# Mamba2 + SwiGLU on one core: four of the eight whole gate/value tiles of block 0 go to three parts, weight passes spread over three engines, a new step order

## The chip, the cores and the metric

One core of one Trainium2 chip runs the whole program as a single launch. The metric is the device time of that launch in microseconds (us); the time before is 364.84 us, the median of three runs (364.48 to 365.87). The engines are named as in the profile: PE (TensorE matmul), PEld (its weight loads), DVE (VectorE), ACT (ScalarE), POOL (GpSimd), SP (SyncE, which issues nearly all loads and stores).

## The reference

Two stages, fp32 in and out. The first is a Mamba2 state-space scan over 4 batches, 8 heads, 768 steps; the second is a SwiGLU feed-forward over the 3072 resulting rows.

```python
# scan, per batch and head; D = 32, N = 16, chunks of 32
log_a = np.log(np.clip(a, 1e-6, 1.0)); cum = np.cumsum(la)           # within a chunk
L = np.exp(cum[i] - cum[j]) * causal
y = ((C @ B.T) * L) @ x  +  (C @ state) * np.exp(cum)
state = np.exp(sum(la)) * state + sum_j(B_j x_j * exp(cum[-1] - cum[j]))
# feed-forward, x = y as (3072, 256); w_gate, w_val: 256 x 1536; w_out: 1536 x 256
xn  = x / sqrt(mean(x*x) + 1e-6) * rms_g
out = (silu(xn @ w_gate) * (xn @ w_val)) @ w_out
```

## The kernel before

**Tiling.** The 3072 rows are 6 blocks of 512 columns (`blk` 0 to 5), each made of two pairs (`p`) of two 128-step chunks. For each block the scan comes first (`gb` products of C and B, `L` decays times products, `A` and `S` the states, `yi` and `ya` the outputs), then the norm (`sq`, `ms`, `rs`, `xn`), then the feed-forward: for each of 12 slices `f` of 128 hidden rows a gate tile (`m` = 0) and a value tile (`m` = 1), each 128x512 in one PSUM bank, `silu` on ACT and `hid` on DVE, and the output products `O`.

**Whole and split tiles.** A tile can be made in two ways. `F` (`gv_whole`, line 1149) multiplies the fp32 weight by the fp32 activation: two matmuls in the program, which the profile records as four. `X` (`gv_split`, line 1159) multiplies three reduced-precision (fp32r) parts: `xh` with `wh`, `xl` with the low half of `wp`, `xk` with the mixed half of `wp`, two matmuls each, six in all. `X` needs six tiles made beforehand: three parts of the activation (`xH`, `xL`, `xK`) and three of the weight (`wH`, `wL`, `wM`). The set `GV4` lists the tiles of block 0 that are whole; besides them slices 0 and 1 of block 0 are made early from the un-normed activation (`early`, line 1112). Block 0's output products (`OF`, line 1234) are all whole, those of other blocks (`OX`, line 1228; `OY`, line 1206) are split.

**Weights.** A piece `k` of the weights (0 to 11 gate and value, 12 to 17 output) is loaded as 16-bit words (`fetch`, on SP) and rebuilt in fp32: `pow` makes a power of two on ACT (two instructions, line 272), `man` makes the mantissa on DVE (line 300), `wt` puts them together on DVE (line 306). Then the parts: `wH` on ACT (line 328) or `wHv` on DVE (line 331), `wL` and `wM` on DVE (line 322).

**The order of the work.** There is no scheduler. One string, `order`, of 1200 steps is written out by hand or by a program outside; each step calls the function of its name and so appends its instructions to the queues of its engines. Each engine takes its queue strictly in that order and waits on semaphores. Steps read `group:name.numbers`: `b:X.0.7.0` is the split gate tile of block 0, slice 7. A step names its engine by its ending: `xL` DVE, `subp` and `hLp` POOL, `hH` ACT, `hHv` DVE.

**Buffers.** `Ring` hands out places of one pool in the order in which they were freed (`free.pop(0)`), at build time. The PSUM banks are the ring `one`, eight of them. So which earlier step a tile must wait for, to get its bank, also follows from the order string.

**The place around the change.** After the common first 150 steps PE makes whole tiles of block 0, the products `gb.1` of pairs 2 and 3, the state products `A.2` and `A.3` (line 830, which read the loaded `x` of pairs 2 and 3 and the scaled `Bd`, and write two PSUM banks each), and the outputs `yi`, `ya` of these pairs (line 916). `Td.3` (`turned_decayed`, line 734, DVE) multiplies a transposed tile by the decays `dT` that SP loads (line 722); it is also the last reader of the bank of `turn.3`.

Of the kernel before, what the change touches and what calls it, by code (L numbers as in the profile page):

```python
# [50 lines left out]
def kernel(  # L51
# [12 lines left out]
    nc = tc.nc  # L64
# [237 lines left out]

    def weight(k):
# [13 lines left out]
    def weight_part(k, i):  # L317

        shape = fetched[k][2]
        if k not in low_parts:  # L320
            split_parts(k)
        nc.vector.scalar_tensor_tensor(  # L322
            out=(low_parts, mixed_parts)[i][k], in0=high_parts[k], scalar=(-UP, GAIN)[i],
            in1=view(ws[k], shape), op0=ALU.mult, op1=(ALU.add, ALU.subtract)[i])
        ws[k].used()
# [40 lines left out]
    kinks = const.tile([P, 2], FP32, name="kinks")  # L366
# [60 lines left out]
    def kinks_of_powers():  # L427
        for k, v in enumerate((-896.0, -1792.0 * 128.0)):
            nc.vector.memset(kinks[:, k:k + 1], v)
# [237 lines left out]
    def scale(p):  # L667
# [3 lines left out]
        for name, src, d in (("Cd", "C", to_i), ("Bd", "B", from_j))[0 if p < 2 else 1:]:  # L671
            s[name + "b"] = k1.take(1, name)
            s[name] = view(s[name + "b"], [P, 2, NH, N])
            nc.vector.tensor_tensor(
# [52 lines left out]
    def turned_decayed(p):  # L727
        if p in SQUARES:
            T = transposed(p)[:, :, 3]
            nc.vector.tensor_tensor(out=T, in0=T, in1=st[p]["dT"], op=ALU.mult)  # L730
# [340 lines left out]
    def x_part(blk, t, i):  # L1071

        xparts[blk, t, i] = b = h.take(modes(blk).count(3), "x" + "hlk"[i])
        part_of(view(b, [P, TB], F32R), xns[blk][1][:, t], view(xparts[blk, t, 0], [P, TB]), i)
# [12 lines left out]
    GV4 = {(0, 2, 0), (0, 3, 0), (0, 4, 0), (0, 4, 1), (0, 5, 0), (0, 5, 1), (0, 6, 0), (0, 7, 0)}  # L1087
# [228 lines left out]
    def token_out():  # L1316
# [23 lines left out]
        "pow": power, "man": mantissa, "wt": weight,  # L1340
        "wH": lambda k: weight_high(k, by_scalar),
        "wHv": lambda k: weight_high(k, by_vector),
        "wL": lambda k: weight_part(k, 0), "wM": lambda k: weight_part(k, 1),
        "open": opened, "early": products_early, "norm": normed, "silu": silu_of, "hid": hidden,
# [10 lines left out]
        "bc": load, "x": load_x, "scale": scale, "turn": turn,  # L1355
# [4 lines left out]
        "dT": spread_decays, "Td": turned_decayed,  # L1360
        "spread": spread, "sub": subtract, "subp": lambda g: subtract(g, pl), "ex": exponential,
# [11 lines left out]
        "xL": lambda blk, t: x_part(blk, t, 1), "xK": lambda blk, t: x_part(blk, t, 2),  # L1373
# [30 lines left out]
        i:early.1.0 i:norm.0 p:Tt.2.0 p:T.3 p:Tt.3.1 i:wHv.2 b:xH.0.0 i:man.5 p:Tt.3.0 i:wL.2  # L1404
        b:F.0.2.0 p:scale.3 i:early.1.1 p:scale.2 i:norm.1 i:ca.2 b:gb.1 b:exps.2 b:L.1.1 i:man.4
        b:L.1.2 b:L.1.3 i:silu.0 i:fetch.10 b:L.1.0 i:man.3 i:gains b:xK.0.0 i:pow.4 i:pow.5
        b:F.0.6.0 b:F.0.7.0 i:silu.1 b:silu.0.7 i:man.12 i:wt.4 b:F.0.3.0 i:pow.3 p:Td.3 p:A.2
        i:wt.5 i:hid.1 b:silu.0.2 b:silu.0.6 i:wt.3 p:A.3 b:F.0.5.0 p:S.2 i:pow.12 i:pow.10
        i:fetch.9 i:fetch.7 i:fetch.14 b:F.0.4.0 p:S.3 b:xHv.0.1 i:wt.12 p:yi.2 i:man.10 p:ya.2
        p:yi.3 b:silu.0.5 i:man.8 i:wt.10 p:ya.3 i:pow.7 i:man.7 b:silu.0.4 i:hid.0 p:qc.4  # L1410
        p:spread.11 i:wHv.3 i:fetch.15 i:wt.7 i:pow.8 b:F.0.4.1 b:OF.0.1.0 b:silu.0.3 b:sq.1.1
        i:wHv.10 b:yt.1.1 b:xL.0.0 i:wM.3 i:fetch.11 b:yt.1.0 p:spread.10 b:OF.0.0.1 i:wt.8 b:xL.0.1
        b:OF.0.0.0 i:wL.10 i:wM.10 b:xK.0.1 p:spread.9 b:OF.0.1.1 b:sq.1.0 i:wH.7 b:F.0.5.1 i:wL.7
        p:qc.5 i:wM.7 b:X.0.11.0 b:sqa.1 i:wL.3 i:pow.14 b:hid.0.4 b:X.0.7.1 i:wHv.8 i:fetch.13
        b:X.0.2.1 i:man.15 i:wH.5 i:man.14 b:table.5 b:hid.0.7 b:X.0.3.1 b:ms.1 i:fetch.17 p:qb.4
        i:pow.11 i:pow.15 i:wM.8 i:man.11 i:wL.8 b:X.0.6.1 b:rs.1 b:hid.0.3 p:subp.10 b:X.0.9.0
        b:hid.0.5 b:X.0.8.0 i:pow.13 i:wt.11 i:wt.14 b:hid.0.6 i:pow.9 i:man.9 i:wt.15 i:man.13
# [137 lines left out]
```

## Time and profile before

| what | value |
|---|---|
| median of three runs | 364.84 us (364.48 to 365.87) |
| the profiled execution's own time | 364.29 us |
| its span, first to last instruction | 362.5 us |
| PE busy | 356.3 us, 3301 matmuls |
| DVE busy | 275.3 us, 514 instructions |
| ACT busy | 183.9 us, 323 instructions |
| POOL busy | 74.8 us, 79 instructions |
| granted TensorE clock | 1.00 throughout |
| DMA, q1, share of 16 engines over the span | 32.8% |

The profiled execution's time is 1.79 us over its span. Busy times are means over stages: DVE is busy 5.00 of 5.00 us in each slice from 60 to 95 us, and well under that after 150 us. Matmuls overlap in the pipeline, so the time that one takes from the one behind it is the distance between starts and not the recorded length; the chain of work gives it, since there a group lasts until the next one begins. "x4" behind a whole tile in the chain is its four records, "x6" a split tile.

### The profile page before, as it was taken

The page shows a single profiled execution, that of the slowest core. Times are in us where ns is not written, and L with a number is a line of the kernel's source. Part 1 is how long each engine was busy: PE and PEld are TensorE (multiplying, and loading weights), DVE is VectorE, ACT ScalarE, POOL GpSimd, SP SyncE. Part 2 cuts the span into 40 slices and gives each one's busy share as a digit, 9 for nine tenths or more (in the row PEclk, how much of TensorE's full clock was granted, in tenths as well). Part 3 has the DMA queues.
Part 4 walks back from the last instruction along what each step waited for, and adds up shares of the span by engine and source line. Part 5 has one row for each costly group of instructions (what it writes and reads, how often), then busy time and mean ns, then how long its engine had stood idle before and what let it go on. Part 6 is the DMA issues. An engine that isn't in the chain of part 4 may idle for free.

```text
span 362.5 us, 8200 instructions
## 1 busy us (share of the span) xinstructions
PE 356.3 (98%) x3301; PEld 284.0 (78%) x3301; DVE 275.3 (76%) x514; ACT 183.9 (51%) x323; POOL 74.8 (21%) x79
## 2 busy tenths in 40 slices
PE   8999989999999999999999999999999999999996
PEld 5667467888787888788788788788788888888886
DVE  6899998999999999872787884696457446629591
ACT  3879878697288946563236755225811121231110
POOL 4022004124011036212102626010010000511140
PEclk9999999999999999999999999999999999999999
DMA  8889968367525224423302031200101000100004
GB/s 103 187 140 288 272 193 224 107 151 117 103 85 137 44 40 103 103 54 85 60 12 81 7 88 31 45 0 4 36 0 31 1 0 2 29 0 2 0 7 110
DMA packets 94702, 27.95 MB, mean 77 GB/s; under 512 B 77545, under 2 KB 92617, under 8 KB 94665
## 3 DMA queue, kind: packets, MB, share of 16 engines
q1 hardware_dynamic: 92584, 27.30, 32.8%
q8 instruction: 26, 0.43, 0.5%
q10 hardware_dynamic: 2080, 0.13, 0.4%
q14 instruction: 12, 0.09, 0.1%
HBM read 23.68 MB, written 3.74 MB: 76 GB/s over the span
## 4 chain that ended last, share of the span: by engine, by line
PE 95%; DVE 2%; issue 1%; POOL 1%; ACT 0%; POOLq 0%; DVEq 0%
PE gv L1159 50%; PE o L1228 18%; PE o L1234 7%; PE gv L1149 4%; PE y L916 3%; PE o L1206 2%; PE gv L1112 2%; PE g L765 2%; PE A L830 1%; PE g L758 1%; PE y L891 1%; PE e L609 1%; POOL hl L1080 1%; PE ms L1014 0%; DVE hk L1082 0%
## 5 line engine op out<-in xcount | busy, mean ns | idle before, releaser
L1159 PE MATMUL gv<-xh,wh 128*128 128x512 f32 x264 | 84.8, 402 | 0.0
L1159 PE MATMUL gv<-xl,wp 128*128 128x512 f32 x264 | 81.5, 390 | 0.0
L1159 PE MATMUL gv<-xk,wp 128*128 128x512 f32 x264 | 81.4, 389 | 0.0
L272 ACT ACTIVATE hx<-gv 128x512 f32<-128x512 f32 x70 | 40.1, 595 | 75.3 <-PE gv L1159 36.5
L1080 POOL TENSOR_TENSOR hl<-hx,hh 128x512 fp32r<-128x512 f32 x27 | 39.5, 1473 | 172.4 <-PE o L1228 105.8
L1174 DVE SCALAR_TENSOR_TENSOR hx<-gv,hx 128x512 f32<-128x512 f32 x70 | 46.6, 683 | 26.9 <-PE gv L1159 19.3
L1159 PEld LDWEIGHTS gv<-xl,wp 128*128 128x128 f32 x264 | 49.6, 188 | 10.6
L1159 PEld LDWEIGHTS gv<-xk,wp 128*128 128x128 f32 x264 | 49.6, 188 | 10.6
L1159 PEld LDWEIGHTS gv<-xh,wh 128*128 128x128 f32 x264 | 48.6, 188 | 10.5 <-issue 0.6
L1082 DVE SCALAR_TENSOR_TENSOR hk<-hx,hh 128x512 fp32r<-128x512 f32 x60 | 47.1, 792 | 8.9 <-PE o L1228 6.0
L328 ACT ACTIVATE hh<-hx 128x512 fp32r<-128x512 f32 x35 | 21.8, 629 | 43.2 <-PE o L1228 20.3
L1228 PE MATMUL o<-hh,wh 128*128 128x512 f32 x96 | 38.0, 396 | 0.0
L1228 PE MATMUL o<-hl,wp 128*128 128x512 f32 x96 | 37.4, 390 | 0.0
L1228 PE MATMUL o<-hk,wp 128*128 128x512 f32 x96 | 37.4, 389 | 0.0
L1080 DVE TENSOR_TENSOR hl<-hx,hh 128x512 fp32r<-128x512 f32 x33 | 24.1, 744 | 5.3 <-PE o L1228 3.7
L631 POOL TENSOR_SCALAR_AFFINE_SELECT L<-L 64x512 f32<-64x512 f32 (+1 forms) x22 | 18.7, 851 | 45.8 <-ACT L L272 45.0
L322 DVE SCALAR_TENSOR_TENSOR wp<-wh,w 128x512 fp32r<-128x512 f32 x36 | 26.3, 756 | 1.0 <-ACT wh L328 1.0
L1234 PE MATMUL o<-w,hx 128*128 128x256 f32 x96 | 23.0, 381 | 0.0
L1228 PEld LDWEIGHTS o<-hh,wh 128*128 128x128 f32 x96 | 18.0, 188 | 4.3 <-issue 0.4
L1228 PEld LDWEIGHTS o<-hk,wp 128*128 128x128 f32 x96 | 18.0, 188 | 3.8
L1228 PEld LDWEIGHTS o<-hl,wp 128*128 128x128 f32 x96 | 18.0, 188 | 3.5
L1234 PEld LDWEIGHTS o<-w,hx 128*128 128x128 f32 x96 | 18.0, 189 | 3.4 <-issue 0.4
(180 smaller groups left out, 504.3 us busy)
## 6 DMA issues: line engine op xcount, KB each, us to landing
L<-rowd SPq DMA_DIRECT2D x32, 128.0 KB
x<-in_x_dram SPq DMA_DIRECT2D x24, 128.0 KB
wr<-in_moe_w_out_dram SPq DMA_DIRECT2D x6, 511.5 KB
wr<-in_moe_w_gate_dram SPq DMA_DIRECT2D x5, 511.5 KB
wr<-in_moe_w_val_dram SPq DMA_DIRECT2D x5, 511.5 KB
out_dram<-ob SPq DMA_DIRECT2D x32, 64.0 KB
bc<-in_B_dram SPq DMA_DIRECT2D x23, 64.0 KB
bc<-in_C_dram SPq DMA_DIRECT2D x23, 64.0 KB
```

Source lines behind the costliest of these rows:

```text
L272: nc.scalar.activation(**operands)
L322: nc.vector.scalar_tensor_tensor(out=(low_parts, mixed_parts)[i][k], in0=high_parts[k], scalar=(-UP, GAIN)[i], in1=view(ws[k], shape), op0 ...
L328: nc.scalar.activation(out=out, in_=in_, func=AF.Copy, scale=scale)
L631: nc.gpsimd.affine_select(out=L[r], in_=L[r], pattern=[[0, L.shape[1]], [1, HC]], compare_op=ALU.is_ge, fill=0.0, base=0, channel_multipli ...
L916: nc.tensor.matmul(out=o[first:first + n, (p % 2 * 2 + i) * HC:(p % 2 * 2 + i + 1) * HC], start=not groups & opened, stop=True, skip_group ...
L1080: engine.tensor_tensor(out=out, in0=v, in1=high, op=ALU.subtract)
L1082: nc.vector.scalar_tensor_tensor(out=out, in0=v, scalar=REST, in1=high, op0=ALU.mult, op1=ALU.subtract)
L1149: nc.tensor.matmul(out=o, lhsT=view(ws[k], fetched[k][2])[:, t, f % 2 * P:][:, 0:P], rhs=xn[:, t], start=(t == 0), stop=(t == 1))
L1159: nc.tensor.matmul(out=o, lhsT=weights_of(m, t, f)[part], rhs=view(x, [P, TB], F32R), start=(part == t == 0), stop=(part == 2 and t == 1))
L1174: nc.vector.scalar_tensor_tensor(out=v, in0=o, scalar=gain(blk, f), in1=v, op0=ALU.mult, op1=ALU.mult)
L1228: nc.tensor.matmul(out=o, lhsT=w[:, b * P:(b + 1) * P], rhs=v, start=opens, stop=True, skip_group_check=True)
L1234: nc.tensor.matmul(out=o[:, j * DM:(j + 1) * DM], lhsT=v[:, tk], rhs=w, start=opens, stop=True, skip_group_check=True)
```

## The change

Four things change; the rest of the code stands as it was.

1. `GV4` shrinks from eight tiles to four: gate tiles 2, 3, 4 and 5 of block 0 stay whole; gate tiles 6 and 7 and value tiles 4 and 5 are split.
2. New steps put old work on other engines: `mana` makes the mantissa on ACT (7 of the 18 pieces), `wMp` makes the mixed part on POOL as high minus low (9 of 18), `scalep` (5), `Tdp` (3) and `xLp` (6 of 12) do `scale`, `Td` and `xL` on POOL. In the other direction `hLp` falls from 27 to 23, `subp` from 7 to 5, `hH` on ACT from 35 to 30.
3. `kinks` gets a third column with 2^23, the bias of `mana`.
4. The order string is the same for its first 150 of 1200 steps and new from there on.

```diff
+    def mantissa_by_scalar(k):
+        words16, u, shape = fetched[k]
+        ws[k] = wb = h.take(3 + uses_whole(k), "w")
+        nc.scalar.activation(out=view(wb, shape), in_=u, func=AF.Identity, scale=2.0 ** -13,
+                             bias=kinks[:, 2:3])
+    def weight_difference(k):
+        shape = fetched[k][2]
+        nc.gpsimd.tensor_tensor(out=mixed_parts[k], in0=high_parts[k], in1=low_parts[k],
+                                op=ALU.subtract)
+        ws[k].used()
-    def scale(p):
+    def scale(p, engine=nc.vector):
-    def turned_decayed(p):
+    def turned_decayed(p, engine=nc.vector):
-    def x_part(blk, t, i):
+    def x_part(blk, t, i, engine=nc.vector):
-    GV4 = {(0, 2, 0), (0, 3, 0), (0, 4, 0), (0, 4, 1), (0, 5, 0), (0, 5, 1), (0, 6, 0), (0, 7, 0)}
+    GV4 = {(0, 2, 0), (0, 3, 0), (0, 4, 0), (0, 5, 0)}
-        i:early.1.0 i:norm.0 p:Tt.2.0 p:T.3 p:Tt.3.1 i:wHv.2 b:xH.0.0 i:man.5 p:Tt.3.0 i:wL.2
+        i:early.1.0 i:norm.0 p:Tt.2.0 p:T.3 p:Tt.3.1 i:wHv.2 i:man.4 i:early.1.1 b:F.0.2.0 i:pow.4
...
```

**PE, first place where the two orders differ, before.** From the last transposes to the outputs of pairs 2 and 3. `gv<-yt` is `early`, `gv<-xn` a whole tile (x2 each), `g` is `gb.1`, `A` is `A.2` and `A.3` together, `y` the outputs.

```order
L1112 MATMUL gv<-yt,w 128x256 x4
L1149 MATMUL gv<-xn,w 128x512 x2
L1112 MATMUL gv<-yt,w 128x256 x4
L765 MATMUL g<-T 64x128 x32
L1149 MATMUL gv<-xn,w 128x512 x6
L830 MATMUL A<-x,Bd 32x64 x28
L1149 MATMUL gv<-xn,w 128x512 x4
L916 MATMUL y<-T,S 64x64 x16
```

The same place after (lines are shifted by 13 or 14).

```order
L1126 MATMUL gv<-yt,w 128x256 x8
L1163 MATMUL gv<-xn,w 128x512 x2
L778 MATMUL g<-T 64x128 x32
L1163 MATMUL gv<-xn,w 128x512 x4
L843 MATMUL A<-x,Bd 32x64 x28
L1163 MATMUL gv<-xn,w 128x512 x2
L1173 MATMUL gv<-xh,wh_601 128x512 x2
L1173 MATMUL gv<-xl,wp 128x512 x2
L1173 MATMUL gv<-xk,wp 128x512 x2
L1173 MATMUL gv<-xh,wh_601 128x512 x2
L1173 MATMUL gv<-xl,wp 128x512 x2
L1173 MATMUL gv<-xk,wp 128x512 x2
```

Between the `early` products and `A` there stood four whole tiles and now three; behind `A` there stood two whole tiles and now one whole tile and two split ones.

**DVE, at `Td.3`, before.** `xk` is `xK`, `w<-wr` is `man`, `w<-w,e` is `wt`, `L` is the decays times products, `T<-tp,dT` is `Td.3`, `A<-A` opens the state step `S.2`.

```order
L788 TENSOR_TENSOR L<-g,L 128x4x128 x3
L300 TENSOR_SCALAR w<-wr 128x512
L477 TENSOR_SCALAR gains<-gcol 128x2
L1082 SCALAR_TENSOR_TENSOR xk<-xn,xh 128x512
L300 TENSOR_SCALAR w<-wr 128x512
L306 SCALAR_TENSOR_TENSOR w<-w,e 128x512
L734 TENSOR_TENSOR T<-tp,dT 128x256
L306 SCALAR_TENSOR_TENSOR w<-w,e 128x512
```

And after.

```order
L801 TENSOR_TENSOR L<-g,L 128x4x128
L1096 SCALAR_TENSOR_TENSOR xk<-xn,xh 128x512
L801 TENSOR_TENSOR L<-g,L 128x4x128
L747 TENSOR_TENSOR T<-tp,dT 128x256
L801 TENSOR_TENSOR L<-g,L 128x4x128 x2
L1096 SCALAR_TENSOR_TENSOR xk<-xn,xh 128x512
L344 TENSOR_SCALAR wh_756<-w 128x512
L860 TENSOR_TENSOR A<-A,tmask 128x128
```

`Td.3` moved ahead of two of the four `L` steps of block 1, with less work of DVE in front of it. The loads on SP are the same in both programs, in the same order, through the loads of `dT.3` and of `x` for pair 3.

**POOL, behind the mask of pair 2, after.** `xl` is `xLp`, `Bd` `scalep`, `wp<-wh,wp` `wMp`, `L<-L,tok` `subp`.

```order
L644 AFFINE_SELECT L<-L 64x1024 x2
L1094 TENSOR_TENSOR xl<-xn,xh 128x512
L687 TENSOR_TENSOR Bd<-bc,d_sb 128x256
L1094 TENSOR_TENSOR xl<-xn,xh 128x512
L336 TENSOR_TENSOR wp<-wh_601,wp 128x512
L336 TENSOR_TENSOR wp<-wh_958,wp 128x512
L672 TENSOR_TENSOR L<-L,tok 128x512
L336 TENSOR_TENSOR wp<-wh_1102,wp 128x512
```

Before, the mask (line 631) was followed by the sum of squares of block 1 (line 974) and two `subp`; the two-input products of the feed-forward on POOL began with `hl` of block 1.

244 lines of the change are left out of this document (124 added, 120 removed).

## Prediction

> **What bounds the kernel now.** I read the page first, then the waits of PE, then the chain of work, then the stage from 30 to 50 us where the two orders part.
>
> ```profile
> span 362.5 us, 8200 instructions
> ...
> PE 356.3 (98%) x3301; PEld 284.0 (78%) x3301; DVE 275.3 (76%) x514; ACT 183.9 (51%) x323; POOL 74.8 (21%) x79
> ...
> PE   8999989999999999999999999999999999999996
> ```
>
> ```profile
> PE y L916 <- issue: 1.3, 1, 1.3
> PE idle L434 <- DVE warm L476: 1.1, 1, 1.1
> PE o L1206 <- POOL hl L1080: 0.3, 1, 0.3
> ```
>
> PE is busy in 356.3 of 362.5 us, and its waits are three: 1.1 us at the start, 1.3 us inside the first run of small output matmuls, of which the profile names no cause ("issue"), and 0.3 us at the tail. So the time is the sum of what PE does. A change gains what it takes out of that sum and loses each new wait of PE in full, because there is no later slack to absorb it.
>
> **What the whole tiles cost.** The chain from 30 to 50 us shows the stage, and one row from later shows split tiles back to back.
>
> ```profile
> 31.04 1.72 PE gv L1149 x4
> ...
> 35.62 5.35 PE gv L1149 x12
> 40.97 0.72 PE A L830 x49
> 41.69 3.63 PE gv L1149 x8
> 45.32 1.14 PE y L916 x80
> ...
> 159.34 2.72 PE gv L1159 x12
> ```
>
> A whole tile (x4) holds PE 1.72 us. Two split tiles (x12) hold it 2.72 us, so one holds it 1.36 us. Each of the four tiles that change kind saves 0.36 us: **4 x 0.36 = 1.4 us** less PE work. Everything else that PE does is only reordered. The parts of the weights and of the activation that the four split tiles need were made before too, for other tiles; they are only due earlier.
>
> **The state products and their loads.** In the old order PE reaches `A` at 40.97 us. What it waited for there stands in these rows: the weight loads of `A`, the semaphore of that line, the DVE step `Td.3`, and SP's issues of `dT.3` and of `x` for pair 3.
>
> ```profile
> 40.90 0.63 PEld L830 LDWEIGHTS A<-x,Bd 64*32 64x32 f32 x56 [0.76 <-DVE T L734]
> ```
> ```profile
> L830 PEldq EVENT_SEMAPHORE  x2: 51/51/51, 36.9 to 41.0; - x2
> ```
> ```profile
> 40.39 0.40 DVE L734 TENSOR_TENSOR T<-tp,dT 128x256 f32<-128x256 f32 x1
> ```
> ```profile
> 36.15 0.60 SPq L722 DMA_DIRECT2D dT<-rowe  x1
> 36.80 1.08 SPq L205 DMA_DIRECT2D x<-in_x_dram  x2
> ```
>
> The load of `A`'s weights was released by `Td.3`, which ended at 40.79 us; the second semaphore of the line cleared at 41.05 us, and the products ran on. PE itself lost nothing, because the whole tile in front of them ended at 40.97 us. The old order meets its data to within 0.1 us. How long loads take to land in this stage is shown by the queue and by one load that ACT waited for:
>
> ```profile
> q1 hardware_dynamic: 6721, 4.62, 96.2%
> ```
> ```profile
> 20.26 0.47 SPq L241 DMA_DIRECT2D wr<-in_moe_w_val_dram  x1
> ```
> ```profile
> 25.02 0.78 ACT L272 ACTIVATE e<-wr,kinks 128x512 f32<-128x512 int16 x1 [0.26 <-DMA wr<-in_moe_w_val_dram]
> ```
>
> From 30 to 46 us the load queue takes 96.2% of the 16 DMA engines. A load issued at 20.26 us was usable at 25.02, 4.76 us later. The second `x` load of pair 3, issued in the second half of the 1.08 us behind 36.80, at about 37.3, would by that be there at 42.1; the line's semaphore had cleared by 41.05. I take 41.05, the row of the load's own reader, though that row does not say whether the reader still waited then; had it been there long before, there would be no wait at all (the first rival). `dT.3`, issued at 36.15, was there by 40.39, when `Td.3` started; by the 4.76 us it would have been at 40.9. I take 40.3.
>
> **The new order at that place.** Through these two loads SP's queue is the same, so they land at the same time. But PE now has three whole tiles and not four in front of `A`, and comes to it 1.72 us sooner, at 40.97 - 1.72 = 39.25 us. `A.2` (24 of the 56 matmuls) can go; `A.3` reads the `x` that lands at 41.05, and the second of its two PSUM banks is the one that `Td.3` frees. So `A.3` ends at about 41.5 and the tile behind it starts at 41.5, where before it started at 41.69. PE waits about 1.5 us there. It cannot go round: `A.3` stands ahead of the next tile in its queue.
>
> The sum from there: the remaining work of PE is what it was from 41.69 to the end, less the 1.4 us, plus the 1.72 us of the whole tile that the old order had already done by then. That is **+0.3 us**; with the start 0.1 to 0.2 us earlier the end comes at **+0.1 to +0.2 us**. So the gain of 1.4 us is eaten by one wait for a load.
>
> **DVE behind it.** On DVE `Td.3` has moved ahead of two `L` steps, an `xK`, the state steps and the next weights, all of which now wait for `dT.3` too.
>
> ```profile
> 36.60 1.88 DVE L788 TENSOR_TENSOR L<-g,L 128x512 f32<-128x512 f32 x3
> 38.40 0.42 DVE L300 TENSOR_SCALAR w<-wr 128x512 f32<-128x512 uint32 x1
> 38.73 0.16 DVE L477 TENSOR_SCALAR gains<-gcol 128x2 f32<-128x2 f32 x1
> ```
>
> ```profile
> 39.74 0.75 DVE L306 SCALAR_TENSOR_TENSOR w<-w,e 128x512 int16<-128x512 int16 x1
> ...
> 42.57 0.41 DVE L847 TENSOR_TENSOR A<-A,tmask 128x128 f32<-128x128 f32 x2
> ...
> 45.19 0.42 DVE L331 TENSOR_SCALAR xh<-xn 128x512 fp32r<-128x512 f32 x1
> ```
>
> Three `L` steps take 38.40 - 36.60 = 1.8 us, 0.6 each (other two-input passes of 128x512 the same), a mantissa 38.73 - 38.40 = 0.33 us, a `wt` 40.39 - 39.74 = 0.65 us, and the two state steps together 45.19 - 42.57 = 2.6 us. From `Td.3` at 40.4: the two `L` steps end at 42.0, `xK` at 42.6. The first of the `L` steps frees the bank of the whole tile behind `A.3` at 41.4, just before it is wanted at 41.5; the second that of the first split tile at 42.0, wanted at 43.2. Both hold. Behind them stand a high part, `S.2`, a `wt`, a mantissa, a high part and `S.3`: 3 x 0.33 + 0.65 + 2.6 = 4.2 us, so `S.3` ends at 46.8. PE, after one whole and two split tiles (1.72 + 2.72 from 41.5), starts the outputs at 45.9 and needs `S.3` for the second half of them (behind 96 matmuls; 80 took 1.14 us), at 47.1. That is 0.3 us of cover. I price a miss at 0 to 1 us, and take 0.2.
>
> **The passes that changed engine.** In the stage of the weights DVE is rid of nine mixed parts and two `xL` (11 x 0.6 = 6.6 us), five `scale` of half the size and seven mantissas (12 x 0.33 = 4 us), 10.6 us in all. DVE is not what ends the time in this stage, so its gain shows only as cover for PE. On ACT a mantissa has no row; its nearest is
>
> ```profile
> L328 ACT ACTIVATE wh<-w 128x512 fp32r<-128x512 f32 x10 | 6.0, 625 | 1.4 <-DVE w L306 1.4
> ```
>
> so 7 x 0.63 = 4.4 us on an engine that is busy 51%: from no cost to the 0.63 us of one of them, if one tile should wait for it; I take none, as ACT idles half the time. On POOL the new passes are two-input operations, and before these rows show what such a pair does to DVE beside it:
>
> ```profile
> 59.60 0.68 DVE L1174 SCALAR_TENSOR_TENSOR hx<-gv,hx 128x512 f32<-128x512 f32 x1
> 60.21 1.15 DVE L322 SCALAR_TENSOR_TENSOR wp<-wh,w 128x512 fp32r<-128x512 f32 x1
> 61.28 1.26 DVE L300 TENSOR_SCALAR w<-wr 128x512 f32<-128x512 uint32 x1
> ```
> ```profile
> 59.76 2.50 POOL L659 TENSOR_TENSOR L<-L,tok 128x512 f32<-128x512 f32 x2 [3.44 <-DMA bc<-in_B_dram]
> ```
>
> A pass on POOL takes 1.25 us where DVE takes 0.6. While the two ran, DVE's pass took 1.15 in place of 0.68 and its mantissa 1.26 in place of 0.42 (the row at 38.40): 1.3 us lost in 2.5 us of POOL. Eleven passes of 1.25 and five half ones of about 0.6 are 17 us of new POOL work, so up to 17 x 1.3 / 2.5 = 8.8 us lost by DVE against 10.6 saved. I take the balance as nothing for the end, since DVE was full before too, in all of 60 to 95 us, and PE still never waited:
>
> ```profile
> 60.00:65.00 5.00, 5.00 (x29) 3.72 (x29) 5.00 (x8) 3.57 (x6) 2.26 (x2) 1.00 0.72 229
> ...
> 90.00:95.00 5.00, 5.00 (x23) 4.25 (x23) 5.00 (x11) 1.12 (x2) 0.00 (x0) 1.00 0.74 114
> ```
>
> (the stretch, its length, then busy time of PE, PEld, DVE, ACT and POOL, the granted clock, the DMA share).
>
> [...]
>
> **The tail.** The last three output products now stand behind the copies of the other results, and the last copy is on ACT. No row shows that order. The bounds are -0.3 (PE's one wait there gone) and +0.5 (SP still issuing another store, at about 0.5 us each as in the row of 36.80). I take 0.
>
> **The sum.** The profiled execution took 364.29 us, 0.55 under the median of 364.84. On it: -1.4 (split tiles) + 1.5 (wait of `A.3`) + 0.2 (DVE behind it) = +0.3, so 364.6 and **365.1** on the scale of the median. A measurement of this kernel can tell about 0.5%, 1.8 us; this is no change.
>
> **Rivals.**
>
> *The gain comes through.* If `x` and `dT` land sooner than the rows say (the load queue is shared with loads that the new order issues later), PE does not wait at `A.3` and the 1.4 us stay: 363.4. If the 1.3 us "issue" gap in the outputs goes as well, 362.1, faster. For it: the gap is nobody's wait that the profile names, and it stands inside a run of very short matmuls, where a few instructions' shift could move it. Against it: the same run stands at nearly the same place in the new order (28 matmuls of the stage's tiles ahead of it in place of 24), and the loads have the same queue. 20%, of which half with the gap gone.
>
> *POOL becomes the bound of the block-0 weights: slower.* A split tile's last two matmuls need the mixed part, which for nine pieces now comes from POOL behind the low part, 1.25 us after it in place of 0.6, behind whatever POOL has queued, and with DVE slowed by the same passes. PE needs 1.36 us a tile, so the moment DVE is later than its cover every further microsecond is PE's. It decides if DVE loses more than the 10.6 us that it saves, which the rows put at 8.8. If it loses 12 us, PE waits 1.4 us; if it loses all 17 us of POOL's time, 6.4 us, of which I let half be covered: 3.2. So 365.1 + 1.4 to 3.2, 366.5 to 368.3. 20%, three quarters of it over the bound of 0.5% (366.7). [...]
>
> *The change does less than it says.* If the four tiles gained nothing on PE (the switch between whole and split tiles costing what they save), the `A.3` wait would stand alone: 366.5. The chain speaks against it: two split tiles in 2.72 us, whole ones in 1.72 wherever they stand. 4%, within 0.5%.
>
> **Chances and range.** My forecast has 56%, all within 0.5%; of the first rival half is within and half faster (10%); of the second a quarter is within and 15% slower; the third is within. For the new order past 50 us, which I have not priced step by step and whose new waits can only add, I move 4% from same to slower. That is faster 0.10, same 0.71, slower 0.19. The range reaches down to the first rival's 363.4 and a little under it, and up to the lower half of the second: 363.0 to 367.3.
>
> **What would show it.** In the changed kernel's profile PE's waits should have a row for `A` (L843) of 1.2 to 1.6 us near 39.5 to 41, released by the `x` load or by `Td` (L747), the first in the list beside the "issue" gap; whole tiles 16 records and split ones 816 (136 x 6); PE busy 354.9 us, 1.4 less. DVE should show an idle of 1 to 2 us ahead of L747. The forecast is wrong if no such wait is there, if waits of PE for POOL or DVE between 50 and 100 us add up to more than 1 us, or if PE is late again after 100 us.

## The result, and the profile after

The changed kernel took 362.84 us (median of six runs, 362.05 to 363.63) against 364.73 us of the kernel before beside it; the ratio is 0.9946, interval [0.9926, 0.9966]. Run again (after_again, below) it took 363.67 us, ratio 0.9965 [0.9942, 0.9988]. So it is faster, by 1.9 us in the first comparison and 1.1 in the second, where the forecast was no change, 365.1 us. Medians in this document are of all runs; the ratios leave out the slow runs, those over 1.5% above the fastest of the same kernel (three of the six of a_dve, one each of a_no_w and a_no_mana).

The page of the changed kernel, its profiled execution being the slowest of the six (363.63 us):

```profile
span 361.9 us, 8231 instructions
...
PE 355.5 (98%) x3309; PEld 285.8 (79%) x3309; DVE 274.0 (76%) x498; ACT 184.0 (51%) x323; POOL 97.0 (27%) x94
...
PEclk9999899999999999999999999999999999999999
```

PE is still busy 98% of the span. One slice, the fifth (36 to 45 us), has a granted clock under full. PE's waits, changed kernel:

```profile
PE A L843 <- DMA x<-in_x_dram: 1.7, 2, 1.5
PE idle L447 <- DVE warm L489: 1.1, 1, 1.1
PE c L570 <- ACT la L272: 0.3, 1, 0.3
PE A L843 <- POOL Bd L687: 0.2, 1, 0.2
```

The first row is the wait that was forecast: `A`, for the load of `x`, 1.5 us and 0.16 us. Two rows of before are gone that the forecast had kept: the 1.3 us "issue" in the outputs and the 0.3 us for `hl` at the tail. PE's timeline at that place, changed kernel (start, length, operation, and in brackets the idle time before):

```profile
38.92 0.43 PE L843 MATMUL A<-x,Bd 64*32 64x64 f32 x24
40.86 0.35 PE L843 MATMUL A<-x,Bd 64*32 64x64 f32 x16 [1.51 <-DMA x<-in_x_dram]
41.37 0.35 PE L843 MATMUL A<-x,Bd 64*32 64x64 f32 x16 [0.16 <-DMA x<-in_x_dram]
41.65 3.62 PE L1163 MATMUL gv<-xn,w 128*128 128x512 f32 x4
...
47.98 0.49 PE L929 MATMUL y<-T,S 32*64 32x64 f32 x32
48.40 0.86 PE L929 MATMUL y<-L,x 64*32 64x64 f32 x64
49.19 0.46 PE L929 MATMUL y<-T,S 32*64 32x64 f32 x24
49.58 0.86 PE L929 MATMUL y<-L,x 64*32 64x64 f32 x64
```

The outputs run through without a gap: 47.98 to 50.4. But the whole tile behind `A` has a row of 3.62 us, where the same tile's row in the second profile of this kernel (after_again) has 1.98. From the start of this tile to the start of the outputs it is 6.33 us here and 4.66 there. The stretches (busy time of the engines, then the clock) say why:

```profile
40.00:42.00 2.00, 0.98 (x33) 0.74 (x34) 1.74 (x4) 1.97 (x4) 0.00 (x0) 0.96 0.57 116
42.00:44.00 2.00, 2.00 (x3) 0.67 (x2) 1.93 (x8) 1.97 (x4) 0.00 (x0) 0.50 1.00 368
44.00:46.00 2.00, 2.00 (x6) 1.14 (x5) 1.97 (x7) 1.59 (x4) 0.00 (x0) 0.68 1.03 341
```

The clock was granted at 0.50 behind the wait, for 3.41 us, and PE lost half of that, 1.7 us. That row belongs to this one execution; four of the other five runs had a mean clock of 1.000 and one 0.999.

### The profile page after: what moved, and what is told of

The parts are those of the page before. It is cut to its first block, busy times and chain, and to the rows that moved or that the text cites. A ratio compares the mean times of both kernels' runs of the same rounds, so it can differ in the third digit from the quotient of the medians.

```text
span 361.9 us, 8231 instructions
## 1 busy us (share of the span) xinstructions
PE 355.5 (98%) x3309; PEld 285.8 (79%) x3309; DVE 274.0 (76%) x498; ACT 184.0 (51%) x323; POOL 97.0 (27%) x94
## 4 chain that ended last, share of the span: by engine, by line
PE 90%; DMA 4%; DVE 2%; SPq 2%; POOL 1%; issue 1%; ACT 0%; POOLq 0%
PE gv L1173 50%; PE o L1242 18%; PE o L1248 7%; PE y L929 3%; PE o L1220 2%; DMA rowd<-r_sb 2%; DMA x<-in_x_dram 1%; PE g L778 1%; PE g L771 1%; DMA L<-rowd 1%; PE A L843 1%; PE gv L1163 1%; SPq L241 1%; PE y L904 1%; PE e L622 0%
## 5 line engine op out<-in xcount | busy, mean ns | idle before, releaser
L1173 PE MATMUL gv<-xh,wh 128*128 128x512 f32 x272 | 87.2, 402 | 0.0
L1173 PE MATMUL gv<-xl,wp 128*128 128x512 f32 x272 | 83.9, 390 | 0.0
L1173 PE MATMUL gv<-xk,wp 128*128 128x512 f32 x272 | 83.8, 389 | 0.0
L1094 POOL TENSOR_TENSOR hl<-hx,hh 128x512 fp32r<-128x512 f32 x23 | 36.0, 1574 | 108.0 <-PE o L1242 28.3
L1173 PEld LDWEIGHTS gv<-xh,wh 128*128 128x128 f32 x272 | 51.0, 189 | 11.8 <-issue 0.9
L1173 PEld LDWEIGHTS gv<-xk,wp 128*128 128x128 f32 x272 | 51.1, 188 | 10.8
L1094 DVE TENSOR_TENSOR hl<-hx,hh 128x512 fp32r<-128x512 f32 x37 | 30.8, 838 | 3.9 <-PE o L1242 2.9
L341 ACT ACTIVATE hh<-hx 128x512 fp32r<-128x512 f32 x30 | 18.4, 628 | 24.9 <-PE o L1242 18.3
L336 POOL TENSOR_TENSOR wp<-wh,wp 128x512 fp32r<-128x512 f32 x9 | 13.9, 1552 | 33.6 <-DVE wp L328 22.3
L344 DVE TENSOR_SCALAR hh<-hx 128x512 fp32r<-128x512 f32 x30 | 17.2, 582 | 6.0 <-PE o L1242 5.9
```

The source lines that it names most:

```text
L336: nc.gpsimd.tensor_tensor(out=mixed_parts[k], in0=high_parts[k], in1=low_parts[k], op=ALU.subtract)
L341: nc.scalar.activation(out=out, in_=in_, func=AF.Copy, scale=scale)
L344: nc.vector.tensor_scalar(out=out, in0=in_, scalar1=scale, scalar2=None, op0=ALU.mult)
L1094: engine.tensor_tensor(out=out, in0=v, in1=high, op=ALU.subtract)
L1173: nc.tensor.matmul(out=o, lhsT=weights_of(m, t, f)[part], rhs=view(x, [P, TB], F32R), start=(part == t == 0), stop=(part == 2 and t == 1))
```

## The experiments

The theory after the result: the four tiles bring 1.4 us, the wait at `A` costs 1.5 to 2 us and sometimes a dip of the clock, and the 1.3 us gap in the outputs is gone because PE no longer runs out of its own instructions there. The rivals: the gap belongs to the outputs' data; the moved passes are themselves the gain; or they are worth nothing. Medians are given with the ratio to the kernel before in the same comparison, where that took 364.59 to 364.76 us. Where an experiment is said to be so much over the changed kernel, it is over its 362.84 us; over all its 18 runs (363.06) it would be 0.2 us less, and over the 363.67 us of its second comparison 0.8 less.

**The gap.** In the kernel before it stands inside the first output burst:

```profile
45.67 0.79 PE L916 MATMUL y<-L,x 64*32 64x64 f32 x57
47.76 0.31 PE L916 MATMUL y<-L,x 64*32 64x64 f32 x7 [1.30 <-issue]
```

```diff
-    nc.tensor.matmul(out=v, lhsT=warm[:, 0:P], rhs=warm, start=True, stop=True)
+    nc.tensor.matmul(out=v[:, 0:72], lhsT=warm[:, 0:P], rhs=warm[:, 0:72], start=True, stop=True)
-        i:idle.7
+        i:idle.23
```

> The kernel before, with 23 idle matmuls of 72 columns at the start in place of 7 of 256: 32 more instructions in PE's stream ahead of everything, about the same time. Theory (the 1.3 us issue gap in the first output burst is PE waiting for its own instructions: in the trace of before an instruction packet of PE is fetched at 45.27 us, just as the burst starts, and the gap stands from 46.24 to 47.76; in the changed kernel the packet comes at 44.03, four us ahead of the burst, and there is no gap): the packet moves some 3 us ahead of the burst, the gap is gone, 1.3 us less, about 363.4, ratio to before 0.9964. Rival (the gap is the burst's own, or a data wait that the profile doesn't name): the gap stays within 0.2 us, 364.7, ratio 1.000. If the shift moves the fetch into another dense burst, a gap of about 1.3 us shows there.

366.28 us, 1.0044 [1.002, 1.0068]. Its timeline of PE, at the first and at the second output burst:

```profile
45.73 0.96 PE L917 MATMUL y<-L,x 64*32 64x64 f32 x64
46.62 0.61 PE L917 MATMUL y<-T,S 32*64 32x64 f32 x24
...
99.80 0.86 PE L917 MATMUL y<-L,x 64*32 64x64 f32 x64
102.39 0.63 PE L1160 MATMUL gv<-xh,wh 128*128 128x512 f32 x2 [1.74 <-DVE Bd L675]
```

The gap is gone from the first burst, and PE ran 1.2 us ahead of before from there to 100 us; then it stood for 1.9 us behind the second burst. The profile puts that wait down to DVE's `Bd` (L675), which ended at 102.27; but the tile that waited does not read it. A packet of PE's instructions had started at 100.09 us, 2.30 us before PE went on. So the gap moved, as the last sentence of the expectation allowed. It did not become a gain, and the forecast of 363.4 failed. The two places account for 0.7 us more in the profiled execution, which took 1.1 us more than that of before; the median lies another 0.9 us above it, with a mean clock of 0.995 in three of the twelve runs.

The same with 11 matmuls of 128 columns, 8 instructions more:

```diff
-    nc.tensor.matmul(out=v, lhsT=warm[:, 0:P], rhs=warm, start=True, stop=True)
+    nc.tensor.matmul(out=v[:, 0:128], lhsT=warm[:, 0:P], rhs=warm[:, 0:128], start=True, stop=True)
-        i:idle.7
+        i:idle.11
```

> The kernel before with 11 idle matmuls of 128 columns at the start in place of 7 of 256: 8 more instructions in PE's stream. In the traces so far PE runs dry at one position of its instruction stream modulo 256 (193: instruction 1217 in before and in a_later_s3, instruction 2497 in b_shift32), when the packet of 256 instructions fetched last was started less than 2.3 to 2.5 us earlier. Theory (PE waits for its own instructions): 8 instructions are four matmuls of 0.43 us, so the fetch starts 1.7 us earlier, at about 43.6, ahead of the first burst, and is there when needed; at the burst of 99 to 102 us, where the shift of 32 had put a new gap of 1.9 us, there is none, since the stream runs dry there 16 instructions of split tiles later. No gap anywhere: 1.4 us less, 363.2, ratio to before 0.996. Rival (the shift of 32 only moved the start and with it everything else): the gap stays in the first burst, ratio 1.000.

364.52 us, 1.0003 [0.999, 1.0015]: the fetch still started at 45.20 us, and the gap stayed, at 1.2 us by the distance between starts. That 8 instructions would move the fetch was wrong. But the gap now stands at another matmul:

```profile
45.65 0.76 PE L917 MATMUL y<-L,x 64*32 64x64 f32 x53
47.42 0.33 PE L917 MATMUL y<-L,x 64*32 64x64 f32 x11 [1.02 <-issue]
```

It comes behind 53 of the 64 and not behind 57. Four matmuls are 8 instructions with their weight loads, so PE stopped at the same place of its instruction stream, though not at the same place of the work. That speaks against the rival that the data of one output are late. The third edit leaves the stream's length alone, in the kernel before:

```diff
-        i:fetch.9 i:fetch.7 i:fetch.14 b:F.0.4.0 p:S.3 b:xHv.0.1 i:wt.12 p:yi.2 i:man.10 p:ya.2
+        i:fetch.9 i:fetch.7 i:fetch.14 p:S.3 b:xHv.0.1 i:wt.12 p:yi.2 b:F.0.4.0 i:man.10 p:ya.2
```

> The kernel before, with the whole tile F.0.4.0 moved from ahead of the first output burst to between its first 32 matmuls (yi.2) and the next 64 (ya.2); the other engines' orders are the same. Theory (the gap is PE out of instructions, and a packet is there 2.2 to 2.5 us after its fetch starts): the burst of small matmuls starts 1.7 us later than its fetch, so the gap of 1.3 us is gone or under 0.3 us, PE waits some 0.4 us for S.2 at yi.2, and the time is 363.3 to 363.7, ratio to before 0.996 to 0.9975. Rival (the gap belongs to the output products themselves, whose data come late): a wait of 1.3 us stays at ya.2, 364.6 or more, ratio 1.000.

364.84 us, 0.9994 [0.998, 1.0008]. The gap shrank to 0.36 us and PE left the burst 0.56 us ahead of before, less than the forecast, because the fetch started at 44.93 us although the burst had started 1.7 us earlier. A gain of that size is inside the interval.

The seven executions that stopped and four that did not, from the packet records of the traces (16,384 bytes each, 26 of them in a run; before has 6,663 records of PE, its weight loads and its semaphores, so a packet is estimated at 256 instructions). The columns: the start of the packet's fetch, the start of PE's last matmul ahead of the stop, the time at which PE goes on, or comes to the position without a stop, the time between the first and the third, and the position in PE's instructions, modulo 256:

```
                fetch starts  last start  goes on    fetch to go-on   position
before             45.27       46.24      47.76         2.49           193
b_shift8           45.20       46.19      47.42         2.23           193
b_split_y          44.93       46.62      47.19         2.26           193
b_spread           45.16       46.46      47.51         2.34           193
a_later_s3         43.97       45.57      46.48         2.51           193
a_s3_pool          45.41       46.74      47.93         2.52           193
b_shift32         100.09      100.44     102.39         2.30           193
no gap: after      44.03         -        48.91         4.88           193
no gap: again      44.14         -        46.93         2.80           193
no gap: a_later    43.98         -        46.59         2.61           193
no gap: a_split_y  44.28         -        46.64         2.35           193
```

In these executions PE stops so only at one position of its stream, and goes on 2.2 to 2.5 us after the packet's fetch started; where PE comes there as late or later (last four rows), it does not stop. In none of the 17 traces does PE pass this position, at any of the packets, sooner than 2.23 us after the fetch started. In the small matmuls of the outputs, some 160 instructions take 1 us (80 matmuls and their weight loads 1.14 us in before), so a fetch that starts with the burst is too late; in tiles they take 18 us and more (a split tile, 6 and 6, takes 1.36 us). That the gap is instruction supply is the author's reading of these rows; no record shows the wait itself. What sets the start of the fetch is open: at this place it comes 2 to 5 us after PE passes the same position one packet before (4.2 us in before, 3.1 in after; in b_shift32 2 us ahead of it), elsewhere mostly under 2 us.

**The tiles.** The old list of eight whole tiles in the changed kernel:

```diff
-    GV4 = {(0, 2, 0), (0, 3, 0), (0, 4, 0), (0, 5, 0)}
+    GV4 = {(0, 2, 0), (0, 3, 0), (0, 4, 0), (0, 4, 1), (0, 5, 0), (0, 5, 1), (0, 6, 0), (0, 7, 0)}
-        b:X.0.7.0 b:X.0.6.0
+        b:F.0.7.0 b:F.0.6.0
```

> The changed kernel with the old list of eight whole tiles (gate tiles 6 and 7 and value tiles 4 and 5 of block 0 are whole again), all else as changed. Theory (the four tiles give 4 x 0.36 us on PE and nothing else of the change depends on them): PE busy 1.4 us more, 364.3, ratio to before 0.9985; PE's wait at the state products stays at 1.5 to 2 us. The tiles ahead of the output burst are 8 instructions of PE fewer than in the changed kernel, so the issue gap may come back: then 1.3 us more, 365.6. Rival (the tiles are worth nothing, since PE waits elsewhere for their parts): 362.8, ratio 0.995.

364.17 us, 0.9973 [0.9949, 0.9996]; 1.3 us over the changed kernel, as the theory had it, but the runs go from 362.2 to 366.1 and the intervals overlap. In its profiled execution `x` landed sooner and PE's wait at `A` was 0.5 us. The timeline shows the tiles apart from that. Here three whole tiles stand ahead of the outputs:

```profile
40.65 5.42 PE L1163 MATMUL gv<-xn,w 128*128 128x512 f32 x12
46.00 0.49 PE L929 MATMUL y<-T,S 32*64 32x64 f32 x32
```

In the changed kernel (after_again) it is one whole tile and two split ones, and this is its first and its last row:

```profile
41.35 1.98 PE L1163 MATMUL gv<-xn,w 128*128 128x512 f32 x4
...
46.01 0.49 PE L929 MATMUL y<-T,S 32*64 32x64 f32 x32
```

That is 5.35 us against 4.66, 0.69 less. At the other two tiles the stretch from the output products ahead of them to those behind takes 4.75 us (from 51.23 in a_whole8) against 4.08 (from 53.22 in after), 0.67 less. So the four tiles bring 1.36 us.

**The wait at `A`, and what is behind it.**

```diff
-        p:A.2 p:S.2 p:A.3 i:wt.3 b:silu.0.4 i:man.5 i:pow.12 b:F.0.5.0
+        p:A.2 p:S.2 i:wt.3 b:silu.0.4 i:man.5 i:pow.12 b:F.0.5.0 p:A.3
```

> The changed kernel with the step A.3 alone moved behind the next whole tile on PE. Theory (PE waits at A.3 for the load of x, 1.5 to 2 us, and nothing else): the wait at A shrinks from about 2 to under 0.4 us, and no dip of the granted clock follows. But S.3 on DVE ends at 46.7 us in the changed kernel, behind wt.3, man.5 and wHv.3, and PE would now come to the second half of the outputs at about 45.4: so most of the gain, 1.3 us, turns up again as a wait of PE for S (L872) or for the outputs' state, and the time is 362.4 to 362.8, ratio 0.9935 to 0.995. Rival (DVE has slack, the wait was all): 361.2, ratio 0.990.

362.98 us, 0.9946 [0.9927, 0.9965]: as the changed kernel. The wait for `x` is gone, and the outputs now wait for DVE's state step:

```profile
PE A L843 <- POOL Bd L687: 0.9, 1, 0.9
PE gv L1173 <- DVE xl L1094: 0.9, 1, 0.9
PE ms L1027 <- DVE sq L987: 0.7, 1, 0.7
...
PE y L929 <- DVE A L860: 0.3, 1, 0.3
```

The 0.3 us of the last row (0.5 by the distance between starts) is less than the 1.3 expected; in this execution, the slowest of the twelve, three later waits, the rows above it, took the rest. Twelve runs showed no clock under 0.999. With DVE's order mended as well:

```diff
-        p:Td.3 b:F.0.3.0 b:L.1.2 p:scalep.2 i:pow.5 b:L.1.0
+        b:F.0.3.0 b:L.1.2 p:scalep.2 i:pow.5 b:L.1.0 p:Td.3
-        p:A.2 p:S.2 i:wt.3 b:silu.0.4 i:man.5 i:pow.12 b:F.0.5.0 p:A.3
+        p:A.2 p:S.2 b:silu.0.4 i:pow.12 b:F.0.5.0 p:A.3 p:S.3 i:wt.3 i:man.5
```

> As a_later, and on DVE Td.3 behind two L steps in place of ahead of them, and S.3 right behind S.2, ahead of wt.3, man.5 and wHv.3. Theory (one wait for a load, then DVE's order behind it): S.3 ends at about 45, both waits go, PE has no wait over 0.4 us up to 60 us; 1.5 to 2.0 us under the changed kernel: 361.0, ratio to before 0.990. Rival (the passes moved back on DVE are due at once, so that a split tile waits for its weight parts): a new wait of 0.5 to 1.5 us for wh or wp (L344, L328) between 45 and 60 us, 362 to 362.8.

362.39 us, 0.9934 [0.9912, 0.9956], 1.4 us short of the forecast. PE came to the outputs sooner, and so the gap came back (a row of PE), and at 107 us PE waited for `Bd`, which POOL made late (two rows of POOL):

```profile
46.48 0.33 PE L929 MATMUL y<-L,x 64*32 64x64 f32 x12 [0.69 <-issue]
...
108.63 0.46 PE L843 MATMUL A<-x,Bd 64*32 64x64 f32 x32 [0.94 <-POOL Bd L687]
```

```profile
106.51 1.04 POOL L672 TENSOR_TENSOR L<-L,tok 128x512 f32<-128x512 f32 x1 [5.42 <-DMA L<-rowd]
107.51 1.07 POOL L687 TENSOR_TENSOR Bd<-bc,d_sb 128x256 f32<-128x256 f32 x1
```

POOL sat 5.4 us behind a load that `subp` wanted, with `scalep` queued behind it. The next kernel changes both:

```diff
-        p:subp.15 b:yt.2.0 ... b:OF.0.8.1 p:scalep.7 b:ms.2
+        p:scalep.7 p:subp.15 b:yt.2.0 ... b:OF.0.8.1 b:ms.2
-        i:idle.7
+        i:idle.11
```

> a_later_s3, with the same 8 instructions more at the start as in b_shift8 (11 idle matmuls of 128 columns), and scalep.7 ahead of subp.15 on POOL (in a_later_s3 POOL sits 5.4 us behind a load that subp.15 wants, with scalep.7 queued behind it, and PE waits 1.15 us at A for what scalep.7 makes). Theory: the gap of 0.9 us at 45.6 to 46.5 goes (fetch 0.9 us earlier), the wait of 1.15 us at 107 to 108 goes, and no wait of PE over 0.4 us is left behind 2 us: 360.3 to 360.8, ratio to before 0.989. Rival (each gain meets the next late piece, the load of subp.15 itself or DVE): 361.5 to 362.4, with a new wait between 105 and 115 us.

362.05 us, 0.9929 [0.991, 0.9948]. The wait at 107 us is gone, so what `scalep` reads had been there; but the gap stayed (1.0 us): as in b_shift8 the 8 instructions did not move it. Last, without them, a split tile between the two parts of the first outputs:

```diff
-        b:X.0.7.0 b:X.0.6.0 i:wHv.3 p:qb.5 b:silu.0.5 i:wL.3 b:silu.0.3 i:man.12 i:fetch.11 p:yi.2
+        b:X.0.7.0 i:wHv.3 p:qb.5 b:silu.0.5 i:wL.3 b:silu.0.3 i:man.12 i:fetch.11 p:yi.2 b:X.0.6.0
```

> a_later_s3 without more instructions at the start, with scalep.7 ahead of subp.15 as in a_s3_pool, and the split tile X.0.6.0 moved from ahead of the first output burst to between its first 32 matmuls (yi.2) and the next 64 (ya.2). In the traces so far PE never went on sooner than 2.23 us after the fetch of the packet that it ran dry of, wherever the fetch started. Theory: the tile, 1.36 us, stands between the start of the fetch and the place where the stream runs dry, so the gap of 0.9 to 1.2 us is gone, and with the wait at A near 107 us gone too the time is 361.0 to 361.4, ratio to before 0.990 to 0.991. Rival (the fetch starts only when the burst of small matmuls itself is under way): the gap stays at 0.7 us or more, 362.0.

361.76 us (361.17 to 362.27), 0.9918 [0.9903, 0.9933]: the fastest kernel here, 3 us under before. PE's waits:

```profile
PE idle L447 <- DVE warm L489: 1.1, 1, 1.1
PE ms L1027 <- DVE sq L987: 0.5, 1, 0.5
PE gv L1163 <- DVE L L801: 0.3, 1, 0.3
```

No gap, no wait for `x`, and the clock at 1.000 in all six runs. The fetch started at 44.28 and PE came to the position at 46.64, 2.35 us later.

**The clock.** PE kept idle longer, by having one whole tile behind `A.3` and not ahead of `A.2`:

```diff
-        p:Td.3 b:F.0.3.0 b:L.1.2 ... p:A.2 p:S.2 p:A.3
+        p:Td.3 b:L.1.2 ... p:A.2 p:S.2 p:A.3 b:F.0.3.0
```

> The changed kernel with the whole tile F.0.3.0 behind A.3 in place of ahead of A.2: PE has nothing to do for 1.7 us more while it waits for x. It tells whether idle time of PE brings the dip of the granted clock. Theory (the clock is halved for 3.4 us when PE idled for some 2 us or more in a stretch; that costs 1.8 us): the wait at A is 3.4 to 3.8 us, most runs show a mean clock of 0.995 or less, and the median is 362.8 + 1.7 + 1.8 = 366.3. Rival (the dips have nothing to do with idle time of PE): clock 0.999 to 1.000 in most runs as in the changed kernel, 364.5.

367.3 us, 1.0057 [1.0032, 1.0082]. In 11 of 12 runs the mean clock was 0.989 to 0.995, and the one with 1.000 took 363.52. Its wait, and two stretches behind it:

```profile
PE A L843 <- DMA x<-in_x_dram: 4.1, 3, 3.5
```

```profile
42.00:44.00 2.00, 1.71 (x33) 0.99 (x34) 2.00 (x5) 1.94 (x4) 0.00 (x0) 0.50 0.76 211
...
46.00:48.00 2.00, 2.00 (x4) 0.89 (x3) 1.91 (x8) 0.56 (x1) 0.00 (x0) 0.50 0.95 289
```

So in these runs the dip came with idle time of PE. The other way round, in the four kernels in which PE waits 0.2 us for `x` or not at all (a_later, a_later_s3, a_s3_pool, a_split_y) none of 30 runs had a mean clock under 0.999. The median is 1 us over the forecast; in the profiled execution the dip lasted 6.83 us, twice as long.

**The moved passes.** All 30 of them back on DVE, at the same places of the order:

```diff
-        "wMp": weight_difference,
-        "mana": mantissa_by_scalar,
-        "scalep": lambda p: scale(p, pl), "Tdp": lambda p: turned_decayed(p, pl),
-        "xLp": lambda blk, t: x_part(blk, t, 1, pl),
+        "wMp": lambda k: weight_part(k, 1),
+        "mana": mantissa,
+        "scalep": scale, "Tdp": turned_decayed,
+        "xLp": lambda blk, t: x_part(blk, t, 1),
```

> The changed kernel with all passes that it had given to POOL and ACT (wMp, scalep, Tdp, xLp, mana) back on DVE, at the same places of the order. Theory of the prediction (what these passes bring is cover that PE does not need): within 0.7 us of the changed kernel, 362.4 to 363.5, ratio to before 0.994 to 0.997. Rival (PE's gains in front come through only because DVE is relieved by some 10 us between 45 and 105 us): waits of PE for DVE (L328, L344, L687 or L1094) of over 2 us in sum between 45 and 105 us, 365 or more, ratio over 1.000.

377.74 us, 1.0285 [1.0249, 1.0321]: about 12 us over the changed kernel by the ratios, the rival's time and more. But of PE's waits only 2.7 us, in three pieces between 45 and 66 us, are the waits for mixed parts that the rival named. Another 3.1 us (at 176.9) stand behind `Td.8`, as in a_no_td below, and 1.8 and 1.7 us are at `A` (40.7 and 117.1). Two dips of the clock cost 3.4 us. Then one kind at a time.

```diff
-        "wMp": weight_difference,
+        "wMp": lambda k: weight_part(k, 1),
-        "xLp": lambda blk, t: x_part(blk, t, 1, pl),
+        "xLp": lambda blk, t: x_part(blk, t, 1),
```

> The changed kernel with the mixed parts (wMp, 9) and the low parts of the activation (xLp, 6) back on DVE, the rest as changed. All the moved passes together were worth 14 us in a_dve. Theory (DVE is full between 40 and 105 us, and PE's new order needs its parts sooner than DVE alone makes them): PE waits for wp or xl (L328, L1094) between 40 and 105 us, 2 to 5 us in sum, and with the dips of the clock that such idle brings 366 to 370, ratio to before 1.003 to 1.014. Rival (the 14 us are made by single waits for loads in DVE's queue, as by Td.8 at 173 us): within 0.7 us of the changed kernel, ratio 0.993 to 0.997.

364.74 us, 1.0013 [0.999, 1.0036]: 1.9 us over the changed kernel, under the 366 that was the least expected. One row of PE carries most of it: the first split tile behind `A` waits for its mixed part, which DVE reached at 44.85 behind `S.2`, where POOL had made it by 39.9 in the changed kernel.

```profile
45.60 0.73 PE L1173 MATMUL gv<-xk,wp 128*128 128x512 f32 x2 [1.81 <-DVE wp L328]
```

```diff
-        "mana": mantissa_by_scalar,
+        "mana": mantissa,
```

> The changed kernel with the seven mantissas (mana) back on DVE, the rest as changed: 7 x 0.33 = 2.3 us more for DVE, between 36 and 105 us. Theory as for a_no_w: a part of these 2.3 us comes out as waits of PE, 363.3 to 365, ratio to before 0.997 to 1.001. Rival: within 0.5 us of the changed kernel, ratio 0.994 to 0.996.

365.59 us, 1.0011 [0.9985, 1.0036], runs from 362.6 to 369.5; 2.8 us by the medians and about 2 by the ratios, with waits for `wp` (1.1 us) and at `A`, and a clock of 0.995 in 4 of 12 runs.

```diff
-        "scalep": lambda p: scale(p, pl), "Tdp": lambda p: turned_decayed(p, pl),
+        "scalep": scale, "Tdp": turned_decayed,
```

> The changed kernel with scale (scalep, 5) and Td (Tdp, 3) back on DVE, the rest as changed. Theory (DVE works strictly in order, so Td.8, which waits for the load of dT, holds up the hidden parts behind it): PE waits 3 us at about 170 us, as in a_dve, and 1 to 2 us at A near 115 us: 366.5 to 368.5, ratio to before 1.004 to 1.010. Rival (only DVE's fill counts, and these are 8 short passes of 0.33 us): 363 to 364, ratio 0.996 to 0.998.

370.03 us, 1.0147 [1.012, 1.0173]: 7.2 us for eight short passes. The row of DVE, the row of PE that came of it, and the row of POOL in the changed kernel:

```profile
163.72 0.43 DVE L743 TENSOR_TENSOR T<-T,dT 128x256 f32<-128x256 f32 x1 [5.77 <-DMA dT<-rowe]
```

```profile
167.89 1.22 PE L1173 MATMUL gv<-xh,wh 128*128 128x512 f32 x2 [3.17 <-ACT hx L272]
```

```profile
164.26 0.93 POOL L743 TENSOR_TENSOR T<-T,dT 128x256 f32<-128x256 f32 x1 [17.73 <-DMA dT<-rowe]
```

The step waits for the load of `dT` on either engine. On POOL 17.7 us of waiting held up nobody; on DVE 5.8 us held up the hidden parts, then `silu`, then PE for 3.2 us, and behind that the clock: PE's first matmuls there took 1.22 us, and the clock was 0.50 for 6.83 us, 3.4 us lost, which the expectation had left out. Ahead of that PE had waited 2.3 us at `A`, since `Bd` of pair 2 now stood on DVE behind `Td.3` (41.93 us); the profile calls this wait "issue" too, so that word alone does not say that instructions were late.

The reverse, the same passes given to POOL and ACT in the old order with the old tiles. The edit is 30 names in the old order string, as in these; seven low and mixed parts change places:

```diff
-        i:man.3
+        i:mana.3
-        p:scale.5
+        p:scalep.5
```

> The old order and the old eight whole tiles, with the same 30 passes given to POOL and ACT as in the changed kernel, each at the place where the old order has it (seven low and mixed parts change places, since the mixed part on POOL is made from the low part). Theory of the prediction (the passes are cover, and PE in the old order waits for nothing that DVE makes): 364.2 to 365.1, ratio to before 0.999 to 1.0015, with the issue gap where it was. Rival 1 (the spread is a gain of its own): 363.5 or less, ratio under 0.997. Rival 2 (POOL works strictly in order and is late where the order was not made for it): waits of PE for POOL over 1 us in sum, 366 or more, ratio over 1.004.

365.75 us, 1.0027 [1.001, 1.0043]: 1.0 us slower, between the prediction's answer and that of rival 2. PE waits 0.5 us for a mixed part from POOL, and the gap is where it was:

```profile
PE y L929 <- issue: 0.8, 1, 0.8
PE gv L1173 <- POOL wp L336: 0.5, 1, 0.5
PE A L843 <- DVE L L801: 0.3, 1, 0.3
```

So the spread is no gain by itself; the new order needs it.

**The changed kernel again.**

> The changed kernel itself once more. All theories: 362.4 to 363.2, ratio to before 0.993 to 0.997; PE's wait at A between 0.8 and 2.1 us from run to run, as x lands, and a dip of the granted clock in fewer than one run in three.

363.67 us (361.46 to 365.50), above what was expected. Six runs with a clock of 1.000 took 361.5 to 363.3 and a seventh 365.5; five with 0.995 took 364.1 to 364.8. Over all 18 runs of the changed kernel the median is 363.06, and six had the dip. Its profiled execution had none, and this first row of PE's waits:

```profile
PE A L843 <- DVE T L747: 1.2, 1, 1.2
```

## Why the prediction was wrong, by its own steps

1. **Split tiles, -1.4 us: right.** By the distance between starts it is 1.36 us (0.69 and 0.67 for two tiles each); undone, the median rose by 1.3.
2. **The wait of `A.3`, +1.5 us: right in place and cause**, and near in size. From the first of these matmuls to the next tile PE took 2.73, 2.41 and 1.73 us in three executions with that order (after, after_again, a_whole8) against 0.72 in before, so it lost 2.0, 1.7 and 1.0 us, as `x` and `dT` landed. What the step left out is that such a wait can halve the clock behind it: 1.7 us more, in 6 of 18 runs. So "eaten by one wait for a load" held for the tiles' gain.
3. **The gap, kept at its 1.3 us: the step that failed.** The sum left the "issue" gap of the outputs where it was, because "the same run stands at nearly the same place in the new order"; only half of the first rival's 20% went to its going. The place is nearly the same, but what counts is when PE comes there: in the changed kernel the packet's fetch starts at 44.0 to 44.1 us and PE comes to the position 2.8 to 4.9 us later, against 1.0 us in before. That took 1.5 us out, by the distance between starts. It is not independent of step 2: the wait at `A` stands ahead of this place and holds PE back by 1.7 to 2.0 us, and with that wait gone the gap was back (0.9 us in a_later_s3). So the forecast's own wait helped to remove the gap that the forecast kept. That the fetch also started 1.1 to 1.2 us sooner than in before is as much a part of it, and its cause is open.
4. **The tail, taken at 0 with a bound of -0.3: the lower bound was nearer.** The wait for `hl` is gone, 0.5 us by the distance between starts (351.99 to 352.60 in before, where a matmul takes 0.12), a little more than the bound.
5. **DVE behind `A`, +0.2 us: nothing was lost**, since `S.3` ended at 46.75 and 46.62 us in the two executions (forecast 46.8) and PE came to the outputs that need it at 49.19 and 47.22 (forecast 47.1). That the cover is thin was right: with `A.3` out of the way PE waited for DVE (a_later).
6. **The moved passes, taken at 0: right as a sum, wrong as a reason.** Between 50 and 100 us PE's list has no wait for POOL or DVE in one execution and 0.3 us for `sq` in the other. But "its gain shows only as cover" undersold it: by the ratios the new order is about 12 us slower without any of it, 7 without `scalep` and `Tdp`, 2 without the mixed and low parts or without the mantissas, and the old order with it 1.0 slower. On contention the changed kernel has both cases side by side:

```profile
36.98 1.26 POOL L1094 TENSOR_TENSOR xl<-xn,xh 128x512 fp32r<-128x512 f32 x1
37.06 1.73 DVE L1096 SCALAR_TENSOR_TENSOR xk<-xn,xh 128x512 fp32r<-128x512 f32 x1
...
38.21 1.72 POOL L336 TENSOR_TENSOR wp<-wh,wp 128x512 fp32r<-128x512 f32 x1
...
38.72 0.68 DVE L801 TENSOR_TENSOR L<-g,L 128x512 f32<-128x512 f32 x1
```

DVE's `xK`, both inputs in SBUF, lost 1.05 us to 1.26 us of POOL (alone it takes 0.68, at 41.80); its `L`, one input of which is in PSUM, lost nothing to 1.72 us of POOL (0.68 us; two of them take 1.28 at 40.61, with POOL idle). The average of 1.3 us in 2.5 of POOL that the prediction took fits neither row.

The sum with the measured terms: -1.4 (tiles) - 1.5 (gap) - 0.5 (tail) + 1.0 to 2.0 (`A`) is -2.4 to -1.4 us without a dip, and up to +0.3 with one. The first comparison gave -1.9, the second -1.1. For the profiled executions the sum is too high: it gives -1.7 where the span of after_again is 2.2 us under before, and +0.3 where that of after is 0.6 under. Of these 0.5 and 0.9 us, 0.3 lie ahead of `A`, to which PE came 1.98 us sooner and not only the 1.72 of one tile; the rest no run here explains. The first rival's time with the gap gone, 362.1, came near, but by half of its mechanism: its condition, no wait at `A.3`, did not hold. POOL as the bound did not come true. That DVE loses all 17 us of POOL's time, the upper end of that rival, no run shows; in the four rows of item 6 it lost 1.05 us beside 2.98 us of POOL.

## What to carry to other kernels

Before a stall of unknown cause is kept in a sum, ask what its time hangs on: one that is a race between two streams (here a fetch and a burst of tiny matmuls) can vanish or move when anything ahead of it shifts. When a step is moved to another engine, look first at what it waits for and at what is queued behind it there; that was worth more than its busy time. And price a wait of the matrix engine with the clock that it may cost behind it, not by its length alone.

## What the runs showed of the hardware

- In seven executions PE stopped at position 193, modulo 256, of its instructions and went on 2.23 to 2.52 us after the fetch of a packet of them began; in none of the 17 traces did it pass that position sooner than 2.23 us after the fetch. From start to start it cost 0.6 to 1.9 us, and the profile shows it as "issue", or blames an engine that had just finished (DVE `Bd` in b_shift32).
- An idle stretch of PE of 1.5 and 0.16 us, with 0.35 us of work between, was followed by a clock of 0.5 for 3.41 us in one execution (1.7 us lost), and not in another with 1.2 and 0.2 us; with 3.5 us of idle it came in 11 of 12 runs.
- The same loads land up to 1 us apart from run to run: in three executions with the same order PE's wait at `A` was between 0.5 and 1.7 us in the profile, and the matmuls behind it went on between 39.85 and 40.86 us.
